# Block sums for the next pair, issued some steps sooner at the change of pairs

## The chip, the core and the metric

The kernel runs on one core of a Trainium2 chip. The metric is the device time of one execution in microseconds (us). The engines of the core run side by side, each in its own order of instructions, and wait for one another through semaphores: PE multiplies matrices into PSUM, DVE (the vector engine) and Pool work elementwise, ACT (the scalar engine) copies and evaluates functions, SP issues most of the transfers.

## What is computed

There are eight batch entries. In each, eight heads of 512 tokens and 32 states attend to one another, tokens to states and states to tokens. The result, 512 numbers for every token and every state, goes through a gated layer:

```python
a = softmax(x @ state.T / sqrt(D));   xread = a @ state      # tokens read states
a2 = softmax(state @ x.T / sqrt(D));  sread = a2 @ x         # states read tokens
h = concat(xread, sread) @ w_in                              # 512 -> 2048
out = (h * cos(h)) @ w_out                                   # 2048 -> 512
```

All arithmetic is in 32-bit floats. The two weight matrices arrive as 64-bit numbers and are converted on the chip during the first part of the run.

## The kernel before

**Steps.** A loop over `all_tiles` does one step for each of the 16 tiles `f` of 128 hidden features of each of the eight entries `b`: steps 0 to 127, with `step = 16 b + f`. Sixteen further steps do the states' rows. In a step PE first makes the hidden tile `h` (line 471, or line 507 as below), ACT and DVE then gate it (`gate` line 560, `gate2` line 563, `gate3` line 566, `gate4` line 573), and PE multiplies a gated tile from three steps before with the second weight matrix (`output`, line 617; `LAG = 3`). Attention for the next entry is spread over the steps by `plan(b)`: its scores, softmax, products and transposes have fixed steps and fixed places on their engines.

**The hidden product.** `xread` is never made. The kernel forms the products of the states with `w_in` (`products`, line 319, copied to `sw` at line 445, each `sw` tile for four steps) and multiplies the attention weights `aT` with them. In odd entries that is two full products at line 471.

**Seven products.** In the entries 2, 4 and 6 (`seven(t)`: an even entry, not the first) two tiles are made at once with seven products of quarter blocks instead of eight. This needs sums of blocks beforehand:

- `halves(b)`, line 488: four DVE subtractions of 128x256 blocks of `aT` into `aS`, once for an entry.
- `sw_sums(t)`, line 502: four Pool additions or subtractions of 128x128 blocks of `sw`, three into `swS` and the last over a block of `sw` itself, once for two tiles.

`hidden_a` makes the first four products (line 507) in the step *before* the first of the two tiles: `b11` of `sw` with `aT`, then `swS[1]` with `aS[1]`, then the block of `sw` written in place with `aS[2]`, then `swS[0]` with `aS[0]`. `hidden_b` makes the last three in the first tile's own step. `sums_a` and `sums_b` add the parts on DVE.

**PSUM.** The hidden tiles rotate through two PSUM buffers named `h` (`hps`, `bufs=2`). An ordinary tile takes one, `hidden_a` takes both. In the step ahead of the first seven-product tile of an entry, the ordinary tile made just before still sits in one of them, so ACT copies it out (line 948) and its gate works from the copy.

**Pairs.** Two entries form a pair: 0 and 1, 2 and 3, 4 and 5, 6 and 7. The second matrix product is also done with seven products of blocks, over the pair, and needs differences of gated tiles: `minus`, line 579. In the last eight steps of a pair each step has three of them. In the first pair all three run on Pool; in later pairs one runs on DVE and two on Pool. Two stand after `gate4` (`sums`), the third at the end of the step (`sums2`). Pool also makes sums of blocks of `w_out` (line 905) in steps 16 to 22 and in steps 32 and 33.

**The change of pairs.** It falls at the steps 32, 64 and 96. Call the first step of the new pair u. Since `hidden_a` for step u runs in step u-1, its block sums are issued at the end of step u-2: first `halves` on DVE, then `sw_sums` on Pool, between that step's second and third `minus`. The `aT` that `halves` reads is complete since `norm1` in the tenth step of the odd entry (u-7). The `sw` block that `sw_sums` reads is copied by ACT in step u-3 (`prod(13, b + 1, 0)` in `plan`).

Of the kernel before, what the change touches and what calls it, by code (L numbers as in the profile page):

```python
# [21 lines left out]
def kernel(  # L22
# [15 lines left out]
    NF = Dff // P  # L38
# [144 lines left out]
    def fetch(n):  # L183
        nonlocal n_fetched
        while n_fetched < n:
            dst, src = loads[n_fetched]
            if f64:
                m, w = dst.shape[1:]

                at_, c0 = (n_fetched - 2) % 3, 0  # L190
                if n_fetched < 4:
                    at_, c0 = n_fetched // 2, n_fetched % 2 * 2 * m * w
                if n_fetched >= N_LOADS:
                    at_ = 3 + n_fetched - N_LOADS
                raw = raw_at[at_].bitcast(I32)[:, c0:c0 + 2 * m * w]
                raw = raw.rearrange("p (m f) -> p m f", m=m)
                nc.sync.dma_start(out=raw, in_=src.bitcast(I32))
                raws[n_fetched] = raw.rearrange("p m (f w) -> p m f w", w=2)
            else:
                nc.sync.dma_start(out=dst, in_=src)  # L200
            n_fetched += 1
# [251 lines left out]
    def part(b, name, *args):  # L453

        if b not in attn:
            attn[b] = Attention(b)
        getattr(attn[b], name)(*args)
        if (name, args) == ("reads", (1,)) and b + 1 < B:
            if b > 0:
                attn[b + 1] = Attention(b + 1)  # L460
                attn[b + 1].load_tokens()
            load_x(b + 1)
# [5 lines left out]
    def hidden(t):  # L468
        t.hp = hps.tile([P, S], F32, name="h")[:, 0:t.n]
        for i in range(t.kn):  # L470
            nc.tensor.matmul(out=t.hp, lhsT=t.lhs(i), rhs=t.rhs(i),  # L471
                             start=(i == 0), stop=(i == t.kn - 1))
# [6 lines left out]
    def seven(t):  # L479
        return t.pair is not None and t.b > 1 and t.phase < 2  # L480

    def halves(b):
        aT = aT_of[b]
        b11, b12 = aT[:, 0, 0:HS], aT[:, 0, HS:S]
        b21, b22 = aT[:, 1, 0:HS], aT[:, 1, HS:S]
        for i, x1, x2 in ((0, b12, b11), (1, b22, aS[:, 0]), (2, b22, b12),
                          (3, b21, aS[:, 1])):
            nc.vector.tensor_tensor(aS[:, i], x1, x2, op=ALU.subtract)

    def blocks_of(t):  # L490
        sw = sw_of[t.b, P * t.f // WC]
        c = P * t.f % WC
        return [sw[:, j, c + P * r:c + P * r + P] for r in range(2)
                for j in range(2)]

    def sw_sums(t):
        b11, b12, b21, b22 = blocks_of(t)
        t1, t2, t4 = [swS[:, i] for i in range(3)]
        sub = ALU.subtract
        for o, x1, x2, op in ((t1, b21, b22, ALU.add), (t2, t1, b11, sub),  # L500
                              (t4, b12, t2, sub), (b21, b11, b21, sub)):
            nc.gpsimd.tensor_tensor(o, x1, x2, op=op)  # L502
# [10 lines left out]
    def both(i1, i2):  # L513

        d = i2 - i1
        ends = slice(i1, i2 + (1 if d > 0 else -1), d)
        return g_all.rearrange("p t (h s) -> p (t h) s", h=2)[:, ends]
# [24 lines left out]
    def hidden_b(t):  # L542
        b11, b12, b21, b22 = blocks_of(t)
        t.h1, t.h2 = [hps.tile([P, S], F32, name="h") for _ in range(2)]
        product_of(t.h1[:, LO], b12, aT_of[t.b][:, 1, LO])
        product_of(t.h2[:, HI], swS[:, 2], aT_of[t.b][:, 1, HI])
        product_of(t.h2[:, LO], b22, aS[:, 3])

    def sums_b(t):
        e, o = 2 * t.slot, 2 * t.second.slot  # L550
        add = nc.vector.tensor_tensor
        add(t.g[:, LO], t.g[:, LO], t.h1[:, LO], op=ALU.add)
        add(both(o, e + 1), both(o, e + 1),  # L553
            t.h2.rearrange("p (h s) -> p h s", h=2), op=ALU.add)
# [14 lines left out]
    def gate4(t):  # L569
        if not hasattr(t, "slot"):  # L570
            t.slot = g_free.pop(0)
            t.g = g_all[:, t.slot, 0:t.n]
        nc.vector.tensor_tensor(t.g, t.hp, t.q, op=ALU.mult)  # L573
# [191 lines left out]
    def tiles():  # L765
        pr = None
        for b in range(B):
            if b % 2 == 0:
                pr = Pair(b // 2, pr)
            for f in range(NF):  # L770
                t = Tile()
                t.b, t.f, t.pair = b, f, pr
                t.phase, t.i = b % 2 * 2 + f // NH, f % NH
                t.n, t.kn = S, 2
                c = slice(P * f % WC, P * f % WC + P)
                t.lhs = lambda i, b=b, nt=P * f // WC, c=c: (
                    sw_of[b, nt][:, i, c])
                t.rhs = lambda i, b=b: aT_of[b][:, i]
                yield t
        for n in range(NF):  # L780
            t = Tile()
            t.b, t.n_th, t.f = B, n, (n + NH) % NF
            t.pair, t.last_pair, t.phase = None, pr, None
            t.n, t.kn = B * Ns, NK
            cols = slice(P * t.f, P * t.f + P)
            t.lhs = lambda i, cols=cols: w_in[:, i, cols]
            t.rhs = lambda i: sT[:, :, Ns * i:Ns * i + Ns]
            yield t


    def warm(n, to):

        for _ in range(n):
            nc.tensor.matmul(out=to, lhsT=zeros[:, 0:P], rhs=zeros, start=True,
                             stop=True)
# [123 lines left out]
    all_tiles = list(tiles())  # L919
    for step, t in enumerate(all_tiles):  # L920
        s = step % NF
        if s == 0 and t.b < B:
            steps = plan(t.b)
        todo = [p[s] if t.b < B else [] for p in steps]

        def go(n):
            for p in todo[n]:
                part(*p)

        last, conv = conv_at.get(step - 1, -1), conv_at.get(step, -1)  # L930
        if step == B * NF + (0 if f64 else 8):
            fetch(N_LOADS + 2)
        if step == 4:
            warm(1, acc[MAIN][0])
        ahead = all_tiles[step + 1:step + 3]
        if seven(t):
            if t.f % 2 == 0:
                hidden_b(t)
                sums_b(t)
        elif step != 1:  # L940
            hidden(t)
        first = len(ahead) > 1 and seven(ahead[0]) and ahead[0].f % 2 == 0
        if first:
            if not seven(t):

                h = t.hp
                take_slot(t)
                nc.scalar.copy(t.g, h)
            hidden_a(*ahead)
        if step == 0:  # L950
            hidden(all_tiles[1])
            warm(3, acc[MAIN][0])
            gate(t)
            gate2(t)
            convert(3, "bcdf")
            convert(4, "1")
            go(0)
        else:
            go(0)
            if step == 5:  # L960
                states(1, acc[SIDE][1])
            if not (seven(t) and t.f % 2):
                gate(t)
            gate2(t)
            if step == 3:
                warm(4, acc[MAIN][0])
                part(0, "products", 1, SIDE)
            if first:
                sums_a(ahead[0])
            go(1)  # L970
            go(3)
            if step == 1:
                convert(4, "bcdf")
            elif last >= 0:
                convert(last, "bcdf")
            if conv >= 0 and not todo[1]:
                convert(conv, "1")
        gate3(t)
        if seven(t) and t.f % 2 == 0:
            gate(t.second)  # L980
        if step == 3:
            part(0, "products_kept", 1, SIDE)
        if later:
            later.pop(0)()
        gate4(t)
        if conv >= 0 and todo[1] and step > 0:
            convert(conv, "1")
        if t.pair is not None:
            sums(t)
        if step == 6:  # L990
            states_kept(1, acc[SIDE][1])
        go(2)
        if conv >= 0:
            convert(conv, "2")
        go(4)
        if step in block_at:
            blocks(*block_at[step])
        for u in all_tiles[step + 2:step + 3]:
            if seven(u) and u.f % 2 == 0:
                if u.f == 0:  # L1000
                    halves(u.b)
                sw_sums(u)
        if t.pair is not None:
            sums2(t)
        while len(line) >= (LAG if step >= 2 * NH else LAG + 1):
            output(line.pop(0))
        line.append(t)
# [32 lines left out]
```

## Time and profile before

| What | Value |
|---|---|
| Time, three runs | 773.12, 773.13, 775.3 us (median 773.13) |
| Span of the profiled execution | 772.9 us |
| PE busy | 758.5 us (98%) |
| DVE busy | 486.5 us (63%) |
| ACT busy | 314.1 us (41%) |
| Pool busy | 228.0 us (29%) |
| Mean granted PE clock | 0.996 |

PE is the engine that fills the span, so the time is PE's work plus PE's waits. A busy share says nothing of where the remaining 14 us are; for that one reads the waits of PE, then the stretches of the timeline in which they lie. The starts of PE's instructions are better to count with than their ends, since matmuls overlap and their ends are modelled: two consecutive matmuls of 512 columns start 0.43 us apart when nothing holds them, two of 256 columns 0.21 us. In the timeline a product at line 507 shows as two matmuls (x2), 0.43 us in all. In a group, "[0.47 <-POOL swS L502]" says that the engine stood idle for 0.47 us before it and that Pool's instruction at line 502 ended the wait.

### The profile page before, as it was taken

Reading aid. Unit: us, or ns where it says so; the run is one execution under the profiler, and the core shown is the slowest. Engines: PE = TensorE matmul, PEld = TensorE weight load, DVE = VectorE, ACT = ScalarE, POOL = GpSimd, SP = SyncE. Lnnn points to the kernel's source line nnn. Section 1 sums busy time; section 2 is a strip of 40 time slices with the busy share of each in tenths; the row PEclk is TensorE's granted clock in tenths of the full one; section 3 lists DMA queues with packets and bytes.
Section 4 is the critical chain, followed back from the end, with each engine's and each line's share of the span. In section 5 each row is a group of like instructions: output and inputs, shape, how many; then the busy total and the mean of one; then the engine's idle time right before and its main releaser. Section 6 shows DMA issues by size and latency. Waiting matters only on the chain.

```text
span 772.9 us, 8101 instructions
## 1 busy us (share of the span) xinstructions
PE 758.5 (98%) x2808; PEld 367.6 (48%) x2808; DVE 486.5 (63%) x786; ACT 314.1 (41%) x511; POOL 228.0 (29%) x214
## 2 busy tenths in 40 slices
PE   8998999999999999999999999999999999999997
PEld 3443444445555434445555434445555444455554
DVE  5778776635886558756886558567876546431431
ACT  3887844522363425333362326332443333212212
POOL 2353278866121000753120001661210005510200
PEclk9999999999999999999999999999999999999999
DMA  8595461050012510340104310420100115000021
GB/s 244 167 275 211 127 93 28 11 99 1 4 24 40 97 28 0 53 85 0 21 8 87 51 27 15 69 54 0 28 1 10 19 27 137 0 1 14 14 41 41
DMA packets 161960, 43.52 MB, mean 56 GB/s; under 512 B 153920, under 2 KB 153920, under 8 KB 161920
## 3 DMA queue, kind: packets, MB, share of 16 engines
q1 hardware_dynamic: 161024, 42.49, 25.7%
q10 hardware_dynamic: 768, 0.39, 0.2%
q8 instruction: 22, 0.36, 0.2%
q0 software_dynamic: 128, 0.13, 0.1%
q14 instruction: 18, 0.15, 0.1%
HBM read 34.08 MB, written 8.91 MB: 56 GB/s over the span
## 4 chain that ended last, share of the span: by engine, by line
PE 89%; DVE 4%; POOL 3%; ACT 2%; DMA 1%; issue 1%; SPq 0%; DVEq 0%; ACTq 0%; POOLq 0%
PE o L617 48%; PE h L471 20%; PE h L507 9%; PE at L319 4%; PE o L737 4%; PE at L409 2%; POOL g_all L579 1%; PE o L319 1%; POOL swS L502 1%; PE at L392 1%; DVE q L563 1%; DMA x_b<-in_x_dram 1%; ACT q L560 1%; DVE g_all L573 1%; ACT q L566 0%
## 5 line engine op out<-in xcount | busy, mean ns | idle before, releaser
L617 PE MATMUL o<-g_all,w_out 128*128 128x512 f32 x512 | 236.3, 598 | 0.3 <-POOL w_out L242 0.3
L579 POOL TENSOR_TENSOR g_all<-g_all 128x512 f32<-128x512 f32 x80 | 113.2, 1436 | 247.9 <-DVE g_all L573 247.9
L617 PE MATMUL o<-g_all,s 128*128 128x512 f32 x384 | 178.5, 601 | 0.0
L563 DVE TENSOR_TENSOR q<-q,h 128x512 f32<-128x512 int32 (+1 forms) x93 | 59.4, 639 | 160.2 <-ACT q L560 160.2
L471 PE MATMUL h<-aT,sw 128*128 128x512 f32 x320 | 152.2, 599 | 2.9 <-DVE g_all L573 2.4
L617 PEld LDWEIGHTS o<-g_all,w_out 128*128 128x128 f32 x512 | 93.8, 190 | 118.5 <-issue 114.7
L560 ACT ACTIVATE q<-h 128x512 int32<-128x512 f32 (+1 forms) x93 | 52.0, 559 | 207.2 <-PE h L471 207.0
L566 ACT ACTIVATE q<-q,halfpi 128x512 f32<-128x512 f32 (+1 forms) x144 | 100.7, 700 | 83.4 <-DVE q L563 83.2
L617 PEld LDWEIGHTS o<-g_all,s 128*128 128x128 f32 x384 | 71.4, 191 | 89.4 <-issue 87.2
L471 PEld LDWEIGHTS h<-aT,sw 128*128 128x128 f32 x320 | 60.5, 191 | 80.0 <-issue 66.7
L573 DVE TENSOR_TENSOR g_all<-h,q 128x512 f32<-128x512 f32 (+1 forms) x93 | 59.3, 637 | 35.0 <-ACT q L566 34.6
L560 ACT ACTIVATE q<-g_all 128x512 int32<-128x512 f32 x51 | 31.8, 623 | 91.9 <-DVE g_all L553 91.5
L563 DVE TENSOR_TENSOR q<-q,g_all 128x512 f32<-128x512 int32 x51 | 38.3, 751 | 21.7 <-ACT q L560 21.7
L242 POOL TENSOR_TENSOR w_out<-w_out,s 128x1024 int32<-128x1024 int32 x10 | 23.9, 2391 | 77.5 <-DVE w_out L237 71.3
L573 DVE TENSOR_TENSOR g_all<-g_all,q 128x512 f32<-128x512 f32 x51 | 36.1, 707 | 10.5 <-ACT q L566 10.5
L502 POOL TENSOR_TENSOR swS<-sw 128x128 f32<-128x128 f32 x24 | 12.0, 499 | 81.9 <-PE h L507 66.9
L579 DVE TENSOR_TENSOR g_all<-g_all 128x512 f32<-128x512 f32 x48 | 33.4, 697 | 1.6
L507 PE MATMUL h<-aS,swS 128*128 128x256 f32 x96 | 29.3, 388 | 2.4 <-POOL swS L502 2.4
L445 ACT COPY sw<-at 128x512 f32<-128x512 f32 x50 | 26.7, 587 | 11.0 <-PE at L319 10.6
L507 PE MATMUL h<-aS,sw 128*128 128x256 f32 x96 | 29.0, 384 | 1.4 <-POOL sw L502 1.2
L242 POOL TENSOR_TENSOR w_in<-w_in,s 128x1024 int32<-128x1024 int32 (+1 forms) x10 | 19.3, 1933 | 37.2 <-DVE w_in L237 20.1
L471 PE MATMUL h<-st_all,w_in 128*128 128x256 f32 x128 | 30.2, 379 | 0.0
(103 smaller groups left out, 784.1 us busy)
## 6 DMA issues: line engine op xcount, KB each, us to landing
out_dram<-ot SPq DMA_DIRECT2D x132, 64.0 KB, 2.0
g_all<-in_moe_w_out_dram SPq DMA_DIRECT2D x8, 1024.0 KB, 5.1
g_all<-in_moe_w_in_dram SPq DMA_DIRECT2D x6, 1024.0 KB, 5.3
xT<-in_x_dram SPq DMA_DIRECT2D x96, 64.0 KB, 2.5
x_b<-in_x_dram SPq DMA_DIRECT2D x24, 256.0 KB, 4.7
x_b<-in_x_dram SPq DMA_DIRECT2D x16, 128.0 KB, 4.2
g_all<-in_moe_w_in_dram SPq DMA_DIRECT2D x4, 512.0 KB, 6.0
x_b<-in_moe_w_out_dram SPq DMA_DIRECT2D x1, 1024.0 KB, 5.8
```

The source lines that it names most:

```text
L242: nc.gpsimd.tensor_tensor(bits, bits, e, op=ALU.add)
L319: nc.tensor.matmul(out=(to or at)[j][Ns * k:Ns * k + Ns, 0:n], lhsT=w[D * j:D * j + D, self.b, Ns * k:Ns * k + Ns], rhs=r(slice(D * j, D * ...
L445: (copy or nc.scalar.copy)(sw_of[self.b, nt][:, j, c0:c1], to[j][:, 0:c1 - c0])
L471: nc.tensor.matmul(out=t.hp, lhsT=t.lhs(i), rhs=t.rhs(i), start=(i == 0), stop=(i == t.kn - 1))
L507: nc.tensor.matmul(out=out, lhsT=w, rhs=r, start=True, stop=True)
L560: nc.scalar.activation(t.q.bitcast(I32), t.hp, func=ACTF.Copy, bias=0.25)
L563: nc.vector.tensor_tensor(t.q, t.q.bitcast(I32), t.hp, op=ALU.subtract)
L566: nc.scalar.activation(t.q, t.q, func=ACTF.Sin, bias=halfpi, scale=-TWO_PI)
L573: nc.vector.tensor_tensor(t.g, t.hp, t.q, op=ALU.mult)
L579: engine.tensor_tensor(out, a, b, op=ALU.subtract)
L617: nc.tensor.matmul(out=acc[bank][ch], lhsT=w[:, i, P * ch:P * ch + P], rhs=g.g, start=(i == 0), stop=(i == NH - 1))
L737: nc.tensor.matmul(out=acc[MAIN][i], lhsT=t.g[:, P * i:P * i + P], rhs=w_out[:, :, t.f, :], start=(t.n_th == 0), stop=(t.n_th == NF - 1))
```

## The change

At the first tile of a new pair the block sums are issued sooner. `halves` moves from the end of step u-2 to the end of step u-5, which is after `norm1` of the same entry. `sw_sums` moves from the end of step u-2 to the middle of step u-3, ahead of `gate4` and of that step's `minus`, after the copies of `sw` in the same step. The purpose is that the operands of `hidden_a` in step u-1 stand ready. All other tiles keep their places: `sw_sums` for them stays at the end of the second step before.

```diff
+    def new_pair(t):
+        return t.b % 2 == 0 and t.f == 0
...
                 sums_b(t)
+                if s == NF - 2 and seven(all_tiles[step + 2]):
+                    halves(t.b + 1)
...
             later.pop(0)()
+        for u in all_tiles[step + 3:step + 4]:
+            if seven(u) and new_pair(u):
+                sw_sums(u)
         gate4(t)
...
         go(4)
+        for u in all_tiles[step + 5:step + 6]:
+            if seven(u) and new_pair(u):
+                halves(u.b)
         if step in block_at:
             blocks(*block_at[step])
         for u in all_tiles[step + 2:step + 3]:
-            if seven(u) and u.f % 2 == 0:
-                if u.f == 0:
-                    halves(u.b)
+            if seven(u) and u.f % 2 == 0 and not new_pair(u):
                 sw_sums(u)
```

The diff moves lines: line 502 before is line 507 after, line 507 is 512, line 573 is 578, line 579 is 584, line 617 is 622, line 905 is 910 and line 948 is 955.

## The prediction

> **What bounds the kernel now.** I read the page first: PE is busy 758.5 of 772.9 us, so only PE's waits can be won. Then the list of PE's waits. Of its eight rows these two concern the block sums (total us, times, longest):
>
> ```profile
> PE h L507 <- POOL swS L502: 2.4, 3, 1.5
> PE h L507 <- POOL sw L502: 1.2, 3, 0.5
> ```
>
> Three times each, though the seven-product steps have 24 such products: once at each change of pairs. Next PE's timeline at the second change (u = 64 in the numbering of steps, 341 us on the clock):
>
> ```profile
> 340.76 0.59 PE L507 MATMUL h<-aT,sw 128*128 128x256 f32 x2
> 341.82 0.70 PE L507 MATMUL h<-aS,swS 128*128 128x256 f32 x2 [0.47 <-POOL swS L502]
> 343.01 0.70 PE L507 MATMUL h<-aS,sw 128*128 128x256 f32 x2 [0.49 <-POOL sw L502]
> 343.55 0.59 PE L507 MATMUL h<-aS,swS 128*128 128x256 f32 x2
> 343.98 0.27 PE L425 MATMUL at<-ident,sr 128*128 128x128 f32 x1
> ```
>
> Read the starts. Products follow one another every 0.43 us when nothing holds them (340.76 to 343.98 should be 1.72); it is 3.22, so 1.50 us are lost, more than the idle 0.96, because a restarted matmul also shows 0.70 instead of 0.59. The third change, by the same count, loses 1.49 (509.50 to 512.71). The chain of waits shows why, at the second change:
>
> ```profile
> 338.81 1.77 POOL g_all L579
> 340.58 0.60 POOL swS L502
> ...
> 342.37 0.60 POOL sw L502
> ```
>
> Pool's sums start only when the first `minus` of step u-2 is done, and that waited for `gate4` of the step. They are not late by their length but by their place.
>
> The first change (171 us) loses more: the first product starts at 169.16 and the transpose that follows the four at 173.59, 4.43 instead of 1.72, so 2.71. The eight output matmuls behind take 4.57 instead of 3.44 us (173.81 to 178.38). Why, the table by stages shows (window, length, PE busy, then the other engines, PE clock):
>
> ```profile
> 169.26:172.67 3.41, 1.69 (x7) 0.86 (x6) 1.60 (x2) 1.29 (x3) 3.25 (x6) 1.00 0.01 2
> 172.67:176.09 3.42, 3.42 (x7) 1.82 (x7) 3.02 (x5) 1.09 (x3) 0.69 (x1) 0.50 0.00 0
> ```
>
> PE stood idle for half of the first window, and in the next it got half its clock. And there is a second place, fourteen us on, in the chain of waits:
>
> ```profile
> 175.51 0.61 DVE g_all L573
> 176.12 0.07 issue
> 176.19 3.71 POOL g_all L579 x3
> 179.90 2.33 POOL w_out L905
> 182.24 0.86 POOL swS L502
> ...
> 184.58 0.87 POOL sw L502
> 185.45 0.04 issue
> 185.49 0.70 PE h L507 x2
> ```
>
> From the gate of step 31 Pool works without a pause: three `minus`, a sum of `w_out`, the sums for tile 34. PE waits for the last of these, though only shortly: its product would have started at 185.19 and started at 185.49, 0.41 us lost with the restart.
>
> **What the Trainium skill says.** "TensorE: Matmul & The Clock Gate", Part 1: the array gets half its clock after an idle window of some 3.4 us and the full one after a busy window; the windows run free of the kernel. The trace agrees: 0.50 for 3.41 us after a window idle for 1.72 us, and none after the second change's, idle for 0.96. "SBUF — State Buffer", section "SBUF: two separate sides": DVE and Pool share a port pair that one holds for a whole instruction, also against a DVE operation with two SBUF inputs. The trace agrees: the first `aS` subtraction of change one takes 0.41 us, the next two 1.37 and 1.48 beside two `minus` of Pool.
>
> **The change part by part.** It adds and removes no instruction. The new line behind `hidden_b` asks for a seven-product step two after an even entry's fifteenth step; that belongs to an odd entry, so it never runs. What is left moves four DVE and four Pool instructions at each of three changes.
>
> *`halves` in step u-5.* Its input is two steps old, the readers of `aS` ended sixteen steps ago, so it waits for nothing. DVE is free from 321.59 to 323.76 at the second change (2.17 us) and from 148.03 to 152.16 at the first (4.13). Pool's `minus` run there too. Cost: four times 0.41 is 1.6 us with the port free, 3.3 as measured at 339.37 to 342.64. I take 3.3: at the first change it fits, at the others the next step's gate, `gate2`, `keep` and `gate4` queue behind it for at most 1.1 us. What waits for `gate4` is the hidden product two steps on, through the PSUM buffer: 326.27 to 333.90, a slack of 7.6 us. Cost on the path 0.
>
> *`sw_sums` in step u-3.* It waits for ACT's copies of `sw`, done at 331.58, and takes 2.4 us (340.54 to 342.96), so until about 334.0. Behind it are that step's `minus`, started 333.08 before, now about 0.9 later, ended near 337.0; the next `minus` starts at 338.81. Pool absorbs it. At the first change three `minus` from 161.55 would start near 162.4 and end near 166.1, before 167.21. Cost 0.
>
> *What replaces the waits.* The third product of `hidden_a` needs the second PSUM buffer, which ACT empties at line 948: 341.02 to 341.60. Without waits PE reaches that product at 340.76 + 0.86 = 341.62. So a restart may remain: 0.03 for the semaphore, 0.11 for a first matmul of 0.483 instead of 0.379. I take 0.15 (bounds 0 and 0.3). **Gain at changes two and three: 1.50 + 1.49 - 0.30 = 2.7.** Behind them PE has no wait down to the next change, and the engines that feed it are started by PE's own results, so the gain stays.
>
> *The first change.* PE alone would win 2.71 + 1.13 + 0.41, less 0.15: 4.1. But the Pool chain ahead of tile 34 moves by less. Its head is ACT's copy at line 529, which waited for the second product and would start at 170.2 to 170.3 (behind line 948's end at 170.28) instead of 171.97: 1.7 sooner. `gate2` of step 31 took 1.00 us beside a `minus`; that one now ends near 170.9, so 0.69: 0.3 more. From there three `minus` and the `w_out` sum keep their 3.7 and 2.3. The sums for tile 34 took 3.2 us beside DVE work; two such series elsewhere take 2.4, so 0 to 0.8 more; I take half, as one DVE operation or two will still meet them. Chain: 1.7 + 0.3 + 0.4 = 2.4. PE, 4.1 sooner, waits the difference there: 1.7 us. **Gain 2.4** (2.0 to 4.1). Whether the half clock falls on the first idle or not matters little for this sum, since in the kernel before the Pool chain already took up what a full clock would have saved.
>
> Sum 2.7 + 2.4 = 5.1: 773.13 - 5.1 = **768.0 us**.
>
> **The rivals.**
> - *All is won* (Pool's sums of tile 34 escape the collision and its `minus` run quicker): 4.1 + 2.7 = 6.8, 766.3. Against it: nothing in the change touches the 3.7 + 2.3 us on Pool.
> - *The wait of 1.7 us costs the clock.* It is about the idle time that halved the clock at the first change; if it falls in one window, 3.41 us at half speed lose up to 1.7. Gain 5.1 - 1.7 = 3.4, 769.7. For it: the 1.72. Against it: the wait would be split between the second and third product and over two windows more often than not.
> - *No change.* Something ties the moved sums to their old time or PE meets another buffer at the same moment, at two of the three changes: 1.4 won, less 1 us of disturbance, 772.7. Against it: the copies and `norm1` are earlier by a step or more.
> - *Slower.* The slack of 7.6 us isn't there, because `gate4` is held in a way that I don't see; then the 3.3 us of `halves` stand on PE's path three times, 9.9 against 5.1: 777.9. Against it: two PSUM buffers and a whole step of PE work between.
>
> **How the numbers follow.** Forecast 0.60, all won 0.12, clock lost 0.16, no change 0.07, slower 0.05. The bound of 0.3% is 2.3 us, so under 770.8 is faster: 0.60 + 0.12 + 0.16 = 0.88; same 0.07; slower 0.05. Range: low end from the full gain at the first change with no restart at the others (4.1 + 3.0 + 0.3 = 7.4): 765.7; high end from 2.0 at the first change less 1.7 for the clock, with restarts of 0.3 at the others (0.3 + 2.4 = 2.7): 770.4.
>
> **What would show it.** In PE's waits the two rows quoted are gone for the changes two and three, and one with Pool's sums as releaser remains near 181 us, with 1 to 2 us. The four products of `hidden_a` at the second change start within 1.7 to 2.0 us. `aS` runs some 18 us before its reader and `swS` some 9 us. `minus` of step u-3 starts up to 1 us later and nobody waits. The prediction is wrong if PE waits at line 471 for a late `gate4` in the steps u-4 to u-2, or if the wait near 181 us is absent.

## The result and the profile after

| | before | after |
|---|---|---|
| Median, four runs each | 773.87 us | 769.89 us |
| Range | 773.12 to 775.3 | 769.8 to 770.73 |
| Span of the profiled execution | 772.9 us | 768.0 us |

The ratio is 0.9949, with a 95% interval of 0.9930 to 0.9967: about 4.0 us (0.5%) faster. A single execution spreads by some 2 us or more; in the nine traces of this case such differences lie in the first 165 us (when the input lands, and whether PE gets half a clock near 73 us). For sizes below a microsecond I therefore read segments of the traces further on.

PE's waits after the change, with the same columns as before (total us, times, longest):

```profile
PE h L512 <- POOL swS L507: 1.0, 1, 1.0
...
PE h L512 <- POOL sw L507: 0.2, 1, 0.2
PE h L512 <- ACT g_all L955: 0.2, 1, 0.2
```

The waits for block sums came three times each; now each comes once (at tile 34, 182 us), and a wait for ACT's copy has joined them. PE's timeline at the second change:

```profile
338.44 0.59 PE L512 MATMUL h<-aT,sw 128*128 128x256 f32 x2
338.88 0.59 PE L512 MATMUL h<-aS,swS 128*128 128x256 f32 x2
339.43 0.67 PE L512 MATMUL h<-aS,sw 128*128 128x256 f32 x2
339.94 0.59 PE L512 MATMUL h<-aS,swS 128*128 128x256 f32 x2
340.37 0.27 PE L425 MATMUL at<-ident,sr 128*128 128x128 f32 x1
```

From 338.44 to 340.37 are 1.93 us; it was 3.22, and 1.72 would be free of waits. What is left is the step from 338.88 to 339.43 and the 0.67: the third product waits for the PSUM buffer that ACT empties (its copy at line 955 ended at 339.28), and restarts. At the first change the lines with the remaining waits:

```profile
168.94 0.59 PE L512 MATMUL h<-aT,sw 128*128 128x256 f32 x2
...
170.20 0.67 PE L512 MATMUL h<-aS,sw 128*128 128x256 f32 x2 [0.24 <-ACT g_all L955]
...
171.25 3.60 PE L622 MATMUL o<-g_all,s 128*128 128x512 f32 x8
174.68 0.59 PE L512 MATMUL h<-aT,sw 128*128 128x256 f32 x2
...
182.24 0.70 PE L512 MATMUL h<-aS,swS 128*128 128x256 f32 x2 [1.02 <-POOL swS L507]
183.18 0.70 PE L512 MATMUL h<-aS,sw 128*128 128x256 f32 x2 [0.24 <-POOL sw L507]
...
184.15 3.60 PE L622 MATMUL o<-g_all,s 128*128 128x512 f32 x8
```

The eight output matmuls now take 3.43 us from the first start to the next product (171.25 to 174.68): no half clock. But tile 34 waits at 182 us, more than it did. The chain of waits tells what for:

```profile
173.23 0.61 DVE g_all L578
...
173.92 3.72 POOL g_all L584 x3
177.64 2.82 POOL w_out L910
180.46 0.86 POOL swS L507
...
182.72 0.42 POOL sw L507
...
183.18 1.13 PE h L512 x4
```

It is the Pool chain of the kernel before, from the gate of step 31 on. It starts 2.3 us earlier by the clock; 0.2 of this is only that this execution reached the change sooner, so 2.1 us are won.

### The profile page after: what moved, and what is told of

It is laid out like the page before. It is cut to its first block, busy times and chain, and to the rows that moved or that the text cites. A ratio compares the mean times of both kernels' runs of the same rounds, so it can differ in the third digit from the quotient of the medians.

```text
span 768.0 us, 8094 instructions
## 1 busy us (share of the span) xinstructions
PE 755.9 (98%) x2808; PEld 367.0 (48%) x2808; DVE 487.4 (63%) x786; ACT 314.1 (41%) x511; POOL 227.7 (30%) x214
## 4 chain that ended last, share of the span: by engine, by line
PE 91%; DVE 3%; POOL 2%; ACT 2%; DMA 1%; issue 1%; ACTq 0%; DVEq 0%; POOLq 0%
PE o L622 49%; PE h L471 20%; PE h L512 9%; PE at L319 4%; PE o L742 4%; PE at L409 2%; PE o L319 1%; POOL g_all L584 1%; PE at L392 1%; DMA g_all<-in_moe_w_in_dram 1%; DMA s<-in_state_dram 0%; POOL w_out L910 0%; DVE q L568 0%; ACT q L565 0%; DVE i L333 0%
## 5 line engine op out<-in xcount | busy, mean ns | idle before, releaser
L568 DVE TENSOR_TENSOR q<-q,g_all 128x512 f32<-128x512 int32 x51 | 36.6, 717 | 28.6 <-ACT q L565 28.6
L742 PE MATMUL o<-w_out,g_all 128*128 128x512 f32 x64 | 29.6, 592 | 0.0
```

The lines of the kernel that those rows point to most:

```text
L568: nc.vector.tensor_tensor(t.q, t.q.bitcast(I32), t.hp, op=ALU.subtract)
L742: nc.tensor.matmul(out=acc[MAIN][i], lhsT=t.g[:, P * i:P * i + P], rhs=w_out[:, :, t.f, :], start=(t.n_th == 0), stop=(t.n_th == NF - 1))
```

## The experiments

All are compared in segments of PE's timeline. A segment runs between two matmuls that every kernel has. S1 runs from the first product of `hidden_a` at the first change to the first output matmul behind tile 34's four products (169.16 to 186.46 before, 168.94 to 184.15 after). S2 and S3 run from the first product to the first output matmul at the second and third change. The stretches between and behind them were the same in all nine kernels: 154.3, 165.4 and 260.1 us, each within 0.02. So what a kernel wins behind the first 165 us lies in S1 to S3. There is one trace of each kernel, and its S1 can hold a half clock; of the nine, only that of the kernel before has one there.

| Kernel | S1 | S2 | S3 | sum against before |
|---|---|---|---|---|
| before | 17.30 | 3.33 | 3.33 | |
| after | 15.21 | 2.03 | 2.03 | -4.69 |
| only `halves` moved | 16.66 | 2.83 | 2.83 | -1.64 |
| only `sw_sums` moved | 15.60 | 3.13 | 3.13 | -2.10 |
| `sw_sums` ahead of `minus`, same step | 15.59 | 3.13 | 3.13 | -2.11 |
| after, `w_out` sums moved | 13.42 | 2.03 | 2.03 | -6.48 |
| after, `halves` twice (it loses 0.50 more ahead of S1) | 15.37 | 2.03 | 2.03 | -4.53 |
| before, `w_out` sums moved | 15.20 | 3.33 | 3.32 | -2.11 |
| after, `halves` in step u-3 | 15.22 | 2.03 | 2.03 | -4.68 |

**Only `halves` moved.** The diff against the kernel before:

```diff
         go(4)
+        for u in all_tiles[step + 5:step + 6]:
+            if seven(u) and u.f == 0:
+                halves(u.b)
...
             if seven(u) and u.f % 2 == 0:
-                if u.f == 0:
-                    halves(u.b)
                 sw_sums(u)
```

> Half of the change alone: the four DVE subtractions of `halves` move to step u-5, Pool's `sw_sums` stay at the end of step u-2. My theory: Pool's place is the larger part, but DVE no longer holds the shared port while Pool works through its `minus` and its sums, so at changes two and three the sums end at about 342.2 instead of 342.96 and PE wins 0.8 us each, at the first change 0.4: about 2.0 us, 772.0 where before has 773.9. Rival (each wait simply takes the place of the other, so only both moves together help): 0, 773.9. Rival (DVE's subtractions were the whole cause): all of the 4 us of the full change, 769.9.

Measured: ratio 0.9976 (0.9963 to 0.9990), 1.9 us. Pool at the second change (this execution reaches it some 1.8 us sooner than that of the kernel before):

```profile
336.98 1.77 POOL L579 TENSOR_TENSOR g_all<-g_all 128x512 f32<-128x512 f32 x1 [2.73 <-DVE g_all L573]
338.71 0.45 POOL L502 TENSOR_TENSOR swS<-sw 128x128 f32<-128x128 f32 x1
```

With DVE out of the way Pool's sums take 0.45 us each instead of 0.52 to 0.63, but they still start behind the `minus`. That `minus` keeps its 1.77, and DVE's own `minus` runs beside it (336.94 to 337.63); the expectation had counted on a free port there too. So S2 gains 0.50 instead of 0.8, while S1 gains 0.64 instead of 0.4. The first rival (nothing alone) and the second (DVE was the whole cause) fall: 1.64 us is neither 0 nor the 4.69 of the full change.

**Only `sw_sums` moved.**

```diff
+        for u in all_tiles[step + 3:step + 4]:
+            if seven(u) and u.f == 0:
+                sw_sums(u)
         gate4(t)
...
                 if u.f == 0:
                     halves(u.b)
-                sw_sums(u)
+                else:
+                    sw_sums(u)
```

> The other half alone: `sw_sums` of a new pair move to the middle of step u-3, `halves` stays at the end of step u-2. My theory: the first change wins nearly all that the full change won there (2.1 us), since `aS[1]` was ready at 168.9 anyway; at changes two and three PE then waits for `aS[1]` and `aS[2]`, which DVE finishes at 341.5 and 342.1 or later beside Pool's `minus`, so 0.2 to 1.0 us each: about 3.1 us in all, 770.8 where before has 773.9. Rival (only both together): 773.9. Rival (DVE never mattered): 769.9 as the full change.

Measured: ratio 0.9973 (0.9965 to 0.9982), 2.1 us. S1 gains 1.70 where 2.1 was expected, S2 and S3 only 0.20 each, the low end of the expectation; its total of 3.1 us was too high. PE's wait and DVE's timeline at the second change:

```profile
340.82 0.67 PE L507 MATMUL h<-aS,swS 128*128 128x256 f32 x2 [1.05 <-DVE aS L488]
```

```profile
337.77 1.49 DVE L488 TENSOR_TENSOR aS<-aT 128x256 f32<-128x256 f32 x1
339.30 1.37 DVE L488 TENSOR_TENSOR aS<-aT,aS 128x256 f32<-128x256 f32 x1
```

This is a wait that takes another's place. Pool, free of the sums, runs its two `minus` on end (337.21 for 3.17 us), and DVE's subtractions stand beside them at 1.49 and 1.37 us; the two behind them, with the port free, take 0.41. At the second and third change the two halves of the change are worth 0.50 and 0.20 alone and 1.30 together.

**The sums ahead in the same step.**

```diff
+        for u in all_tiles[step + 2:step + 3]:
+            if seven(u) and u.f == 0:
+                sw_sums(u)
         if t.pair is not None:
             sums(t)
...
                 if u.f == 0:
                     halves(u.b)
-                sw_sums(u)
+                else:
+                    sw_sums(u)
```

> `sw_sums` of a new pair stay in step u-2 but go ahead of that step's `minus` instead of between the second and third; `halves` stays. My theory says it is the place in Pool's queue behind a `minus` that waits for `gate4`, not the step, that made the sums late: Pool is idle before that `minus` (2.7 us at change two, 1.9 at change one), so the sums end before it, and the time equals that of the variant with the sums in step u-3, 770.8, within 0.5 us. Rival (a whole step of lead is needed): 772 to 774.

Measured: ratio 0.9979 (0.9969 to 0.9988), against 0.9973 with the sums in step u-3, and the same segments within 0.01. The time of 770.8 that I gave it was too low, as for the variant it was to equal; that the two agree was the point. At the second and third change the agreement alone would not decide, since PE waited there for DVE's `aS` in both variants (1.05 to 1.06 us). Pool's timeline at the second change does:

```profile
334.73 0.46 POOL L502 TENSOR_TENSOR sw<-sw 128x128 f32<-128x128 f32 x1
336.02 3.18 POOL L579 TENSOR_TENSOR g_all<-g_all 128x512 f32<-128x512 f32 x2 [0.83 <-DVE g_all L573]
```

The last of the sums was done at 335.19. All four ran in time that Pool had spent idle (from 333.25 on), and PE's first product started at 337.98. No product of `hidden_a` waited for Pool at any of the three changes. So it is the place in Pool's queue, behind or ahead of a `minus` that waits for the gate, and not the step.

**The `w_out` sums out of Pool's chain.** Against the changed kernel:

```diff
-                32: (ALU.subtract, s3, a11, a21, lo),
-                33: (ALU.subtract, s3, a11, a21, hi)}
+                17: (ALU.subtract, s3, a11, a21, lo),
+                23: (ALU.subtract, s3, a11, a21, hi)}
```

> The changed kernel, with Pool's two sums of `w_out` that stood in steps 32 and 33 (each 2.3 to 2.8 us, the start of what delays the sums for tile 34) moved to steps 17 and 23, where Pool has gaps. My theory: the wait of 1.0 + 0.24 us with two restarts that is left near 182 us in the changed kernel is the tail of this Pool chain; without it the four products of tile 34 start at 180.63 + 0.43 each and the output matmuls at 182.35 instead of 184.15: 1.8 us less, 768.1 where the changed kernel has 769.9. Rival (tile 34 waits for something else at the same time, such as its PSUM buffer or gate): 769.9. Rival (the moved sums now delay the `minus` of the first pair or the early steps): 771 or more.

Measured: 768.72 us in the median, ratio to before 0.9917 (0.9901 to 0.9932). S1 falls from 15.21 to 13.42, by 1.79, where 1.8 was expected. PE at tile 34:

```profile
181.51 0.59 PE L512 MATMUL h<-aT,sw 128*128 128x256 f32 x2
...
183.24 3.60 PE L622 MATMUL o<-g_all,s 128*128 128x512 f32 x8
```

The four products start 0.43 us apart, with no wait (181.51 to 183.24). The tail at 182 us was Pool's, and its removable part was the sum of `w_out`. All four of its executions (766.88 to 768.89 us) were faster than the fastest of the changed kernel (769.80).

**The same move without the change.** The same two lines, in the kernel before.

> The kernel before, with Pool's two sums of `w_out` moved from steps 32 and 33 to steps 17 and 23, and the block sums where they were. It tells what that move is worth without the change. My theory: PE still waits for the block sums at the first change (2.7 us), and only the tail near 185 us goes; where the half clock falls on the first change that tail was 0.4 us, without it about 1.9 (the Pool chain then takes up what the full clock saves). So 0.4 to 1.9 us less than before's 774.5, 772.6 to 774.1, against 1.8 us under the change. Rival (the move is worth the same in both, independent of the change): exactly 1.8, whatever the clock does. Rival (worth nothing before): 774.5.

Measured: ratio 0.9993 (0.9983 to 1.0003), no difference that can be told from none. Its profiled execution had no half clock, and S1 is 2.10 shorter than that of the kernel before, whose S1 had one (1.9 expected). The single executions go with the clock. With a mean granted clock of 1.000 (to three digits, so no half clock) it took 771.5 and 771.6 us against 773.1 to 773.7 of before. At 0.996 it took 774.3 to 776.1 (median of eight 774.6) against 774.2 to 776.0 (median of eight 775.1). The trace of the kernel before had that same 0.996 from two windows of half clock, one near 73 us and one at the first change; that the others at 0.996 had theirs in the same places is inferred, as they left no trace. So in the kernel before, the 1.8 us are there when the clock is full, and at most some 0.5 when it is halved, which speaks against the rival "the same in both". It is what the prediction said: the Pool chain took up what a full clock would have saved.

**`halves` in step u-3.** One line of the changed kernel: `all_tiles[step + 3:step + 4]` in place of `all_tiles[step + 5:step + 6]`.

> The changed kernel with `halves` at the end of step u-3 instead of u-5. My theory: what counts is that it isn't in step u-2, where Pool's `minus` hold the shared port and PE waits in the next step; in step u-3 it ends about 335, 3.5 us before its reader: 769.9, the same segments as the changed kernel. Rival (the three steps are needed, since the subtractions in u-3 delay `gate4` of u-2 and with it the `minus` and the tail at the first change): 0.5 to 1.5 us more.

Measured: ratio 0.9931 (0.9914 to 0.9949), the segments those of the changed kernel within 0.01. The subtractions took 0.67, 1.37, 1.49 and 0.41 us and ended at 334.3, ahead of their reader at 338.04. So step u-3 is early enough for `halves`, and the lead of three steps isn't needed. Whether a place further ahead in step u-2 would do was not tried.

**`halves` twice.** A second `halves(u.b)` behind the first in the changed kernel.

> The changed kernel with `halves` computed twice in step u-5 (the second time writes the same values again): DVE has 3.5 to 5.2 us more in front of the next step's gate. My theory: `gate4` of step u-4 comes that much later, but what waits for it is the hidden product two steps on; the slack, 7.6 us in the kernel before and 6.4 after the move (`gate4` ends at 325.2, the product starts at 331.6), takes it up: 769.9, no change against the changed kernel. Rival (a gate that late stops PE): up to 5 us at each of three changes, 785, and a wait of PE at line 471 in step u-2.

Measured: 771.06 us in the median of five (769.55 to 772.77), ratio to before 0.9952 (0.9934 to 0.9970). No wait at line 471 came up in step u-2, at any change; S2 and S3 are unchanged. At the first change, though, a wait appeared which the expectation hadn't named:

```profile
160.32 1.09 PE L319 MATMUL at<-w_in,st_all 64*32 64x512 f32 x16 [0.43 <-DVE sr L419]
```

In step u-4 DVE also runs `keep` (line 419), which frees the PSUM tile `at` for the products of step u-3. The eight subtractions, six of them 0.82 to 1.49 us beside Pool, held it. The slack toward this reader is the smaller one: before, `keep` ended at 153.95 and the products started at 157.74. With the restart the wait costs 0.50 us ahead of S1, and S1 is 0.16 longer than in the changed kernel, so the expected "no change" missed by 0.66 us. The rival, up to 5 us at each change, is far off too.

## Why the prediction was right, point by point

- **Place, not length.** That Pool's sums were late because they stood behind a `minus` waiting for `gate4` is shown by the variant that moves them within the step. DVE on the shared port added to it: with `halves` alone out of the way, S2 gained 0.50.
- **Changes two and three: 2.7 us.** S2 and S3 gave 1.30 each, 2.60. The restart left over, put at 0.15, is 0.20 (2.03 where 1.72 + 0.11 would do).
- **First change: 2.4 us.** S1 gave 2.09. Of the 0.4 us by which the segments (4.69) fall short of 5.1, 0.3 lie here. By its terms: the head of the chain to the end of step 31's gate came 2.05 sooner (1.7 + 0.3 predicted), the three `minus` kept 3.72. The mis-sized term is the sum of `w_out`: held at 2.3, it took 2.82 in the chain. It now started 0.04 us behind `gate2` of step 32 on DVE. The timelines, before and after:

```profile
179.87 2.37 POOL L905 TENSOR_TENSOR w_out<-w_out 128x1024 f32<-128x1024 f32 x1
181.26 1.52 DVE L563 TENSOR_TENSOR q<-q,g_all 128x512 f32<-128x512 int32 x1 [0.70 <-ACT q L560]
```

```profile
177.56 0.69 DVE L568 TENSOR_TENSOR q<-q,g_all 128x512 f32<-128x512 int32 x1 [0.70 <-ACT q L565]
177.60 2.86 POOL L910 TENSOR_TENSOR w_out<-w_out 128x1024 f32<-128x1024 f32 x1
179.14 1.87 DVE L578 TENSOR_TENSOR g_all<-g_all,q 128x512 f32<-128x512 f32 x1 [0.89 <-ACT q L571]
```

Before, `gate2` came in the middle of the sum: DVE's instruction was stretched (1.52 us) and Pool's was not. After, `gate2` was first: it kept 0.69, and Pool's sum was stretched by 0.5; `gate4`, which came in the middle of the sum, took 1.87. So which of the two is stretched goes with which starts first; in the five other traces with this sum in step 32 behind `gate2` it took 2.80 to 2.87 us too. The sums for tile 34 gave back 0.53 (3.21 to 2.68; 0.4 predicted). PE's remaining loss, 1.7 predicted, is 1.79.
- **The restart at the first change** was too small at 0.15. The third product started at 170.20 instead of 169.80. ACT's copy began 0.32 us after its own wait had ended, in the kernel before as well as after; at the other changes it began 0.04 us after. The name that the profile gives as releaser differs between the two kernels (PE before, Pool after). The 0.32 is the same in all nine traces, though Pool's `minus` end at different times in them, so that releaser doesn't explain it. The cause stays open. In the changed kernel it cost nothing in the sum, since the Pool chain behind set the end of S1; with the `w_out` sums out of that chain it is most of what was missing to 6.8.
- **`halves` costs nothing at u-5.** Right; `gate2` of the next step came 1.2 us later against PE (1.1 predicted) and nobody waited. But the slack of 7.6 us that I named is not the tightest: `keep` has 3.8, as the doubled `halves` showed.
- **`sw_sums` costs nothing at u-3.** Right: the `minus` behind it started 0.94 us later against PE at the second change (0.9 predicted) and no wait followed.
- **The level.** 768.0 was 773.13 less 5.1. The segments say 4.7. The rest of the difference to 769.89 is put down to the start: 773.13 was a low sample of before, whose median in the four runs is 773.87, and the first 165 us differ from execution to execution. So the measured time stands near the upper end of the range, 770.4.
- **Two slips in the working.** The low end of the range seems to count the 0.30 of the restarts twice: the 3.0 for changes two and three already stands without them, so it should be 766.0. And the readers of `aS` had ended thirteen steps before `halves`, at 254 us, not sixteen. Neither touches the forecast.
- **The rivals.** "All is won" came true only when the `w_out` sums went too (6.48 in the segments, 6.8 predicted), which also shows what stood in its way. "The wait costs the clock" did not happen at 182 us in any profile here; the wait was split between two products, as argued. How close it was, the last section shows.

## What to carry to other kernels

When an engine in order stands idle behind an instruction that waits, work queued behind it that is ready is late by its place; look for such work first. Here moving it cost nothing. How far that goes depends on the slack toward every reader of what the moved work delays, as the doubled `halves` showed with 0.66 us. Two producers of one consumer that get in each other's way are best moved together: here `halves` alone gave 0.50 us, the sums alone 0.20, because the other became the wait, and both 1.30. After a wait falls, follow the chain of the same engine some steps on; there the time that you won may meet the next piece of fixed work, and that piece may be free to move.

## What the runs showed of the hardware

"TensorE: Matmul & The Clock Gate", Part 1, speaks of an idle window and a busy one; the prediction read off 1.72 us of idle time in a window of 3.41 us as enough. The nine traces don't bear that figure out as a limit, but they show how finely the clock can hang on where a window falls. All nine have the same gap near 73 us: PE waits 1.94 to 1.95 us for a gate. In four traces one window held the whole gap, and the next had half a clock; in five the edge of a window cut the gap, the fuller window was idle for 1.78 to 1.92 us, and the clock stayed full. The tables by stages of the changed kernel and of the one with only `halves` moved:

```profile
69.68:73.10 3.42, 1.47 (x5) 0.41 (x3) 3.22 (x6) 3.39 (x6) 0.59 (x1) 1.00 0.44 169
73.10:76.51 3.41, 3.41 (x4) 1.06 (x4) 2.35 (x5) 2.97 (x5) 1.76 (x1) 0.50 0.90 270
```

```profile
70.10:73.51 3.41, 1.50 (x4) 0.38 (x2) 3.31 (x6) 3.38 (x6) 0.48 (x1) 1.00 0.50 195
73.51:76.92 3.41, 3.38 (x21) 1.16 (x22) 2.24 (x5) 3.38 (x6) 1.88 (x1) 1.00 0.67 253
```

Idle time alone doesn't sort the windows, though: 1.72 us at the first change were enough, and 1.98 in the changed kernel's last full window, behind which the clock stayed full, were not. Counting PE's work by starts (0.43 us for a matmul of 512 columns, 0.21 for 256) does somewhat better: the window at the first change was then free for 2.26 us and three of those near 73 us for 2.11, all followed by half a clock, while no window past the first 10 us that was free for less than 2.07 was. Between, it went both ways: of three windows near 2.08, among them that from 179.4 us on (the wait of tile 34) with the sums ahead in the same step, only one was followed by half a clock, and that last window of the changed kernel, free for 2.14, was not. So by this count the limit seems to lie near 2.1 us, and these traces don't fix it further.
